# Random-feature attention and a gated MLP on one core: wider token chunks, and two sweeps over the weights in the second pass

## The chip, the cores and the metric

The kernel runs on one core of a Trainium2 chip. The metric is the device time of one execution in microseconds, as the median of several runs. TensorE (PE) does the matrix products, VectorE (DVE), ScalarE (ACT) and GpSimd (POOL) the element work, and SyncE (SP) issues most of the transfers between HBM and the on-chip memory SBUF. Products are summed in PSUM.

## The reference

```python
def _attn_ref(q, k, v, omega):            # q, k, v: 8 x 8 x 576 x 64, omega: 128 x 64
    def phi(x):
        proj = np.einsum('bhsd,md->bhsm', x, omega)
        h = proj - np.sum(x * x, axis=-1, keepdims=True) / 2.0
        h = h - np.max(h, axis=-1, keepdims=True)
        return np.exp(h) / np.sqrt(m)
    q_p, k_p = phi(q * scale), phi(k * scale)
    kv = np.einsum('bhsm,bhsd->bhmd', k_p, v)
    num = np.einsum('bhsm,bhmd->bhsd', q_p, kv)
    den = np.einsum('bhsm,bhm->bhs', q_p, np.sum(k_p, axis=2))[..., None] + 1e-06
    return num / den

x = attention, laid out as 4608 tokens x 512
gate = 1.0 / (1.0 + np.exp(-(x @ w_gate)))     # 512 -> 1536
val = x @ w_val                                # 512 -> 1536
out = gate * val @ w_out                       # 1536 -> 512
```

All of it is in fp32; the inputs arrive as float64.

## The kernel before

**Precision.** TensorE reads fp32r. Each operand is split into a high part (written by ACT) and a low part (input minus high, by DVE or POOL), and each product is three matmuls: low x high, high x low, high x high.

**Attention** takes some 500 us. It is a set of coroutines that are advanced in turn (`steps`). It leaves x, transposed, in DRAM (`xT`).

**Gated layer.** The 1536 columns are 12 tiles of 128, in 6 pairs. There are two ways of computing them. The *first pass* (`first_pass`, matmuls `gv` at L247) takes the first 4 tiles (pairs 0 and 1) for 9 chunks of 512 tokens, in plain products of 512 columns, 12 matmuls a step, 80 steps. Its steps are filler for attention: after every step attention is advanced RATE = 14 times. What is left of it when attention ends runs by itself. A chunk's operands are `xe`, a step's gate `ge` (ACT) and result `ye` (DVE). The *second pass* (`second_pass`, `gated`, matmuls `gw` at L351) takes the other 4 pairs in seven-product blocks (Strassen-Winograd): for each chunk of 512 tokens, each pair and each kind (gate, value) a *group* of 7 products of 6 matmuls, 256 columns wide. A product runs over one of seven combinations of quarters of x (`xl0` to `xl6`; sums `s3` to `s6` by DVE, high halves by ACT, low halves 0, 3 and 6 by POOL and 1, 2, 4 and 5 by DVE) and one of seven combinations of weights, a *unit* `u`. The sums of products are read from PSUM by ACT (`p1`) and DVE (`u2`, `u3`, `gl`, `yl`), multiplied and recombined by POOL and stored to DRAM as `yl`; the last group's multiplications are DVE's.

**Units.** Weights are converted from float64 during attention (`convert_weights`) and stored in DRAM as fp32 (`w32`), 1 MB each. `unit` loads one in two parts of 3 and 4 blocks and splits it (`u`, 128x768 and 128x1024). Units 0 to 7 of the second pass are all kept in SBUF for its whole length. Units 8 to 13 are the last layer's.

**Last layer** (`last`, matmuls `po` at L465): for 18 rows (c, s) of 2 x 128 tokens, and each pair j, 21 matmuls of 256 columns from `yh` and `yl`, which ACT and DVE split from the loaded `yr`. For pairs 0 and 1 four combinations of `yr` are first made by DVE (L456), since the first pass left plain products. The sums (`p1o`, `u2o`, `u3o`, `o`) are read by ACT and DVE.

**Order.** A scheduler orders each engine's instructions; those in `pin` keep the order in which the program was written. Every engine runs its instructions in order, and so a waiting one holds up those behind it. Buffers come from rings (`bufs=`); an `x` buffer for `xl`, `yh` and `yl` comes from a ring of 13.

Of the kernel before, what the change touches and what calls it, by code (L numbers as in the profile page):

```python
# [48 lines left out]
FROM = 20  # L49
RATE = 14  # L50
# [5 lines left out]
XK, XL = 5, 8  # L56
UL, UE = 5, 3
# [42 lines left out]
def attn_glu_kernel(ctx: ExitStack, tc, qT, kT, qn, kn, va, om, ident, w, out):  # L100
# [64 lines left out]

    def convert_weights(tiles, ns):

        for n in ns:
# [4 lines left out]
            b, t = f[:, :4], f[:, 4:]
            for o, x, y in (
                (t[:, 0], b[:, 3], b[:, 0]),
                (t[:, 2], b[:, 2], b[:, 3]),
                (t[:, 1], b[:, 2], t[:, 0]),
                (t[:, 3], b[:, 1], t[:, 1]),
            ):
                nc.gpsimd.tensor_tensor(out=o, in0=x, in1=y, op=ALU.subtract)  # L180
# [685 lines left out]
```

## Time and profile before

| | us |
|---|---|
| median of 3 runs | 1234.82 (1232.73 to 1238.44) |
| profiled execution | 1239.43 |
| its span in the profile | 1237.6 |

The span runs from the first to the last instruction. In the profile busy TensorE time is the sum of modelled matmul intervals; a group `L351 PE MATMUL gw<-xl,u ... x3024` names line, engine, operation, output and inputs with their count. In a timeline, the bracket `[3.57 <-ACT p L362]` is the idle time ahead and what ended it. The chain of waits is followed back from the last instruction. A window row gives start and end, length, then busy time and number of instructions of PE, weight load, DVE, ACT and POOL, the granted TensorE clock (1 is full), the DMA share and GB/s. TensorE's mean clock was 0.968.

### The profile page before, as it was taken

What the parts mean: (1) busy time and instruction counts of PE and PEld (TensorE: products, weight loads), DVE (VectorE), ACT (ScalarE), POOL (GpSimd) and SP (SyncE); (2) the same over time, 40 slices, a digit from 0 to 9 for tenths busy, and PEclk for the clock granted to TensorE, in tenths of its full rate; (3) what the DMA queues carried; (4) which work ended last, traced back from release to release, by engine and by line L of the source; (5) the groups of instructions that cost most, each with busy time, mean ns of one, the idle gap of its engine ahead of it and who ended that gap; (6) DMA issues with size and microseconds to landing.
All of it is one profiled execution on the core that took longest, in us unless ns stands there. A gap on an engine that the chain in (4) does not pass through costs nothing.

```text
span 1237.6 us, 23990 instructions
## 1 busy us (share of the span) xinstructions
PE 1172.3 (95%) x8828; PEld 1109.8 (90%) x8828; DVE 864.5 (70%) x1907; ACT 530.7 (43%) x1164; POOL 542.7 (44%) x599
## 2 busy tenths in 40 slices
PE   6798989999898999899899999999998899999998
PEld 5788978798887888788899999999998899999998
DVE  4889888999698866433566656666569777777773
ACT  5556755565455463342423322232325344343331
POOL 2454365556457552131466666666666211111110
PEclk7798989999899999899899999999999999999999
DMA  7667767786657641461432333323337676666662
GB/s 247 213 199 228 210 219 253 238 268 237 226 182 252 223 153 39 139 202 52 152 128 106 123 135 124 121 93 125 124 135 267 203 226 195 188 191 189 198 191 94
DMA packets 104950, 219.43 MB, mean 177 GB/s; under 512 B 11136, under 2 KB 42112, under 8 KB 103040
## 3 DMA queue, kind: packets, MB, share of 16 engines
q1 hardware_dynamic: 87984, 198.94, 48.5%
q10 hardware_dynamic: 16848, 18.95, 4.4%
q8 instruction: 70, 1.15, 0.4%
q14 instruction: 48, 0.39, 0.1%
HBM read 141.82 MB, written 76.02 MB: 176 GB/s over the span
## 4 chain that ended last, share of the span: by engine, by line
PE 71%; DVE 12%; issue 7%; DMA 5%; POOL 3%; ACT 1%; SPq 1%; ACTq 0%; DVEq 0%; POOLq 0%
PE gw L351 27%; PE po L465 20%; PE gv L247 10%; PE pkv L595 4%; PE pnq L638 4%; PE ptq L626 2%; DVE mxq L552 2%; DVE hq L615 1%; DMA xr<-xT 1%; DMA xT<-xsq 1%; DMA rawk<-kT 1%; POOL loq L71 1%; DVE hmq L556 1%; PE ppk L547 1%; POOL xe L71 1%
## 5 line engine op out<-in xcount | busy, mean ns | idle before, releaser
L351 PE MATMUL gw<-xl,u 128*128 128x256 f32 x3024 | 364.6, 283 | 6.9 <-ACT p L362 3.6
L351 PEld LDWEIGHTS gw<-xl,u 128*128 128x128 f32 x3024 | 363.5, 191 | 7.9 <-DVE u L331 3.9
L465 PE MATMUL po<-u,yh 128*128 128x256 f32 x1512 | 272.4, 283 | 0.0
L465 PEld LDWEIGHTS po<-u,yh 128*128 128x128 f32 x1512 | 234.8, 191 | 0.0
L465 PE MATMUL po<-u,yl 128*128 128x256 f32 x756 | 214.0, 283 | 3.3 <-DVE yl L71 3.3
L247 PE MATMUL gv<-xe,wh 128*128 128x512 f32 (+1 forms) x640 | 201.0, 388 | 2.1 <-POOL xe L71 2.1
L70 ACT ACTIVATE yh<-yr 128x896 fp32r<-128x896 f32 x108 | 100.2, 950 | 156.8 <-PE po L465 86.3
L465 PEld LDWEIGHTS po<-u,yl 128*128 128x128 f32 x756 | 144.3, 191 | 3.9 <-DVE yl L71 3.9
L247 PEld LDWEIGHTS gv<-xe,wh 128*128 128x128 f32 x640 | 117.3, 194 | 20.1 <-POOL xe L71 4.5
L71 POOL TENSOR_TENSOR yl<-yr,yh 128x896 fp32r<-128x896 f32 x17 | 38.0, 2232 | 215.3 <-PE po L465 139.9
L247 PE MATMUL gv<-xe,wl 128*128 128x512 f32 (+1 forms) x320 | 125.8, 394 | 2.7 <-POOL wl L71 1.6
L71 DVE TENSOR_TENSOR yl<-yr,yh 128x896 fp32r<-128x896 f32 x91 | 103.0, 1144 | 31.5 <-PE po L465 19.1
L331 DVE TENSOR_TENSOR u<-gw,p 128x256 f32<-128x256 f32 x144 | 60.7, 422 | 59.2 <-PE gw L351 51.1
L595 PE MATMUL pkv<-v,kpk 128*128 128x66 f32 x512 | 84.4, 290 | 13.3 <-ACT kpk L587 12.6
L595 PEld LDWEIGHTS pkv<-v,kpk 128*128 128x128 f32 x512 | 77.0, 209 | 21.5 <-ACT kpk L587 19.8
L71 POOL TENSOR_TENSOR lok<-rawk,hik 128x256 fp32r<-128x256 f32 (+1 forms) x80 | 55.5, 712 | 68.0 <-ACT hik L70 67.6
L456 DVE TENSOR_TENSOR yr<-yr 128x128 f32<-128x128 f32 x144 | 60.1, 451 | 35.3 <-DMA yr<-ye 34.8
L71 POOL TENSOR_TENSOR xe<-xr,xe 128x512 fp32r<-128x512 f32 (+1 forms) x40 | 49.1, 1244 | 74.2 <-ACT xe L70 62.4
L71 POOL TENSOR_TENSOR loq<-rawq,hiq 128x256 fp32r<-128x256 f32 (+1 forms) x80 | 56.5, 718 | 55.5 <-ACT hiq L70 54.7
L587 ACT ACTIVATE kpk<-ppk,nb 128x128 f32<-128x128 f32 x256 | 69.8, 393 | 17.4 <-DVE nb L574 17.1
L638 PEld LDWEIGHTS pnq<-kv,qpq 128*128 128x128 f32 (+1 forms) x640 | 70.5, 189 | 6.5 <-ACT qpq L628 4.3
L638 PE MATMUL pnq<-kv,qpq 128*128 128x66 f32 (+1 forms) x640 | 74.9, 273 | 1.4 <-ACT qpq L628 1.2
(108 smaller groups left out, 2166.6 us busy)
## 6 DMA issues: line engine op xcount, KB each, us to landing
yl<-yl SPq DMA_DIRECT2D x36, 896.0 KB, 3.8
yr<-yl SPq DMA_DIRECT2D x72, 448.0 KB, 3.5
xr<-xT SPq DMA_DIRECT2D x68, 256.0 KB, 4.7
c<-w SPq DMA_DIRECT2D x28, 512.0 KB, 5.1
w<-c SPq DMA_DIRECT2D x14, 1024.0 KB, 4.5
v<-va SPq DMA_DIRECT2D x32, 330.0 KB, 3.4
natk<-kn SPq DMA_DIRECT2D x36, 256.0 KB, 4.2
natq<-qn SPq DMA_DIRECT2D x36, 256.0 KB, 3.9
```

Source lines behind the costliest of these rows:

```text
L70: nc.scalar.activation(out=hi, in_=x, func=AF.Copy)
L71: (lo_engine or nc.vector).tensor_tensor(out=lo, in0=x, in1=hi.bitcast(F32), op=ALU.subtract)
L247: nc.tensor.matmul(gv, lhsT=u[:, s], rhs=v, start=(m == 0), stop=(m == 3 * KC - 1))
L331: return nc.vector.tensor_tensor(out=o, in0=a, in1=b, op=ALU.add)
L351: nc.tensor.matmul(o, lhsT=u[:, k, s], rhs=v[:, kc, :], start=(first and m == 0), stop=(m == 5), skip_group_check=not first,)
L456: nc.vector.tensor_tensor(out=raw[:, o], in0=raw[:, a], in1=raw[:, b], op=op)
L465: nc.tensor.matmul(o, lhsT=u[:, i, :], rhs=v[:, k, :], start=(j + m == 0 and n in (1, 6, 5, 4)), stop=(j == NPAIR - 1 and m == 2), skip_gr ...
L552: nc.vector.tensor_reduce(out=m.rearrange("p t h -> p (t h)"), in_=pp, axis=AX.X, op=ALU.max)
L587: nc.scalar.activation(out=kp[t][:, h, :], in_=pp[:, 2 * i + h, :], func=AF.Exp, bias=nb[:, t - t0, h : h + 1], scale=SCALE,)
L595: nc.tensor.matmul(pkv[:, h, :], lhsT=kp[b * MID + i][:, h, :], rhs=v[:, i, h, :], start=(i == 0), stop=(i == MID),)
L626: nc.tensor.transpose(out=pt[:, i, :], in_=h_sb[:, i, :], identity=id_sb)
L638: nc.tensor.matmul(pn[r, 2 * i + h, :], lhsT=qp[:, 2 * i + h, r], rhs=kvs[u, p, bb][:, h, :], start=True, stop=True,)
```

## The change

- The chunk of the second pass is 768 tokens instead of 512 (HC = 384 columns for a matmul, six chunks).
- The second pass is run in sweeps of two pairs each: sweep zero does pairs 0 and 1 on the last two chunks; then pairs 2 and 3, then pairs 4 and 5, each on all six chunks, 56 groups in all. Operands of x are so made 14 times for 768 tokens and not 9 times for 512.
- The first pass stops at 3072 tokens: 56 steps, 672 matmuls, and not 80 and 960.
- Only the four units of a sweep and one more are held. The next sweep's units are loaded in the last four groups of a sweep and split two groups later. Units -4 to -1 for sweep zero are put together again from the first pass's split weights, by POOL during attention (`first_units`), and stored in `w32`.
- Units 9 to 13 of the last layer come in the last four groups and behind them; unit 12 lies in three x buffers (`scattered`).
- RATE is 16 instead of 14, conversions start at first-pass step 14 instead of 20 (FROM), and the last layer has 8 x buffers.

The matmuls of the second pass go from 3024 of 256 columns to 2352 of 384; the last layer has 2268 before and after. Behind the last matmul of attention in TensorE's order stand 318 first-pass matmuls before and 72 after.

```diff
-NCH = B * S // NC
+HC = 384
+SUB = HC // P
+NC2 = B * S // (2 * HC)
+C0 = 4
+NCH = C0 * 2 * HC // NC
-FROM = 20
-RATE = 14
+FROM = 14
+RATE = 16
-XK, XL = 5, 8
-UL, UE = 5, 3
+XL, XT = 8, 4
...
+    def first_units(tiles):
+        for pair in range(EP):
+            for kind in range(2):
+                n = 2 * (pair - EP) + kind
+                f = tiles(f"z{pair}_{kind}")[:, : 4 * WP].bitcast(F32).rearrange("p (b q) -> p b q", q=Q)
+                for o, r, c in ((0, 0, 0), (1, 1, 0), (2, 1, 1), (3, 0, 1)):
+                    wh, wl = (t.bitcast(F32) for t in ws[2 * pair + c])
+                    i = (kind * KC + 2 * r) * P
+                    nc.gpsimd.tensor_tensor(out=f[:, o], in0=wh[:, i : i + Q], in1=wl[:, i : i + Q], op=ALU.add)
+                    if o % 2:
+                        yield
+                sums(f)
+                nc.sync.dma_start(out=w32[n % N_UNITS], in_=f)
+                yield
...
-        raw = load(c * NC, NC)
+        raw = load(c * 2 * HC, 2 * HC, late)
-        a11, a12, a21, a22 = raw[:, :2, :Q], raw[:, 2:, :Q], raw[:, :2, Q:], raw[:, 2:, Q:]
+        a11, a12, a21, a22 = raw[:, :2, :HC], raw[:, 2:, :HC], raw[:, :2, HC:], raw[:, 2:, HC:]
...
-        b0, b1, b2 = (any_bank(f"gw{i}_{id_}")[:, :Q] for i in range(3))
+        b0, b1, b2 = (any_bank(f"gw{i}_{id_}")[:, :HC] for i in range(3))
...
-        for c in range(NCH):
+        chunks = [(c, (j, j + 1)) for j in range(0, NPAIR, 2) for c in range(0 if j >= EP else C0, NC2)]
+        g_ = 0
+        for (c, pairs), after in zip(chunks, chunks[1:] + [None]):
...
-            if j < EP:
+            if j < EP and c < C0:
                 for o, a, b, op in ((3, 7, 2, ALU.add), (4, 3, 0, ALU.subtract), (5, 0, 7, ALU.subtract), (6, 1, 4, ALU.subtract)):
...
-        left = 2 * NE * (NCH + 1) - n
-        started, parts = [], iter(())
-        for n, _ in enumerate(gates):
-            if n == 2:
-                started = [unit(late, n) for n in range(UL)]
...
+        parts = operands(C0)
+        x = next(parts)
+        todo = [unit(late, n) for n in range(-2 * EP, 0)]
+        for one in todo:
+            next(one)
+        for _ in gates:
+            if todo:
+                next(todo.pop(0), None)
+            next(parts, None)
+            next(parts, None)
...
+    NZ, NA = 4 * (NC2 - C0), 4 * NC2
+    homes = {0: (0, tail)}
+    homes.update({NZ - 4 + i + 1: (i + 1, late) for i in range(4)})
+    homes.update({NZ + NA - 4 + i + 1: (i + 5, (tail, late, late, late)[i]) for i in range(4)})
+    homes.update({NZ + 2 * NA - 4 + i + 1: (i + 9, (late, tail, late, None)[i]) for i in range(4)})
+    for g in second_pass(x, parts):
+        if loading and loading[0][0] <= g:
+            next(loading.pop(0)[1], None)
+        if g in homes:
+            n, at = homes[g]
+            one = unit(at, n, both[n % 2]) if at else unit(late, N_LATE - 1, both[1])
+            next(one)
+            loading.append((g + 2, one))
+        if g == last_group - 1:
+            one = scattered(N_LATE - 2, nc.vector, nc.gpsimd, nc.vector)
```

Where the second pass begins, DVE's order before, up to the first reads of a second-pass sum (`u20_2_0`: kind 0, pair 2, chunk 0). Names end in a running number:

```order
L275 SCALAR_TENSOR_TENSOR ye4096_0_7642<-ge4096_0_7622,gv4096_0_1_7629 128x512
L300 TENSOR_TENSOR s0_3_7645<-xr0_0_7624 128x512
L300 TENSOR_TENSOR s0_4_7664<-s0_3_7645,xr0_0_7624 128x512
L275 SCALAR_TENSOR_TENSOR ye4096_1_7682<-ge4096_1_7662,gv4096_1_1_7669 128x512
L300 TENSOR_TENSOR s0_6_7705<-xr0_0_7624,s0_4_7664 128x512
L296 TENSOR_TENSOR xl0_4_7686<-s0_4_7664,xl0_4_7686 128x512
L296 TENSOR_TENSOR xl0_1_7688<-xr0_0_7624,xl0_1_7688 128x512
L275 SCALAR_TENSOR_TENSOR ye4096_2_7724<-ge4096_2_7703,gv4096_2_1_7711 128x512
L300 TENSOR_TENSOR s0_5_7727<-xr0_0_7624 128x512
L296 TENSOR_TENSOR xl0_5_7730<-s0_5_7727,xl0_5_7730 128x512
L275 SCALAR_TENSOR_TENSOR ye4096_3_7763<-ge4096_3_7745,gv4096_3_1_7750 128x512
L296 TENSOR_TENSOR xl0_2_7748<-xr0_0_7624,xl0_2_7748 128x512
```

The same place after (`xl4` belongs to chunk 4, the first of sweep zero; `u-2` and `u-1` are units, `u20_0_4` the first read):

```order
L344 TENSOR_TENSOR xl4_4_7257<-s4_4_7231,xl4_4_7257 128x768
L344 TENSOR_TENSOR xl4_1_7259<-xq3072_0_7179,xl4_1_7259 128x768
L217 TENSOR_TENSOR u-2_7190<-u-2_7190 128x768
L217 TENSOR_TENSOR u-2_7190<-u-2_7190 128x1024
L348 TENSOR_TENSOR s4_5_7286<-xq3072_0_7179 128x768
L212 SCALAR_TENSOR_TENSOR u-1_7193<-u-1_7193 128x768
L212 SCALAR_TENSOR_TENSOR u-1_7193<-u-1_7193 128x1024
L344 TENSOR_TENSOR xl4_5_7289<-s4_5_7286,xl4_5_7289 128x768
L344 TENSOR_TENSOR xl4_2_7292<-xq3072_0_7179,xl4_2_7292 128x768
L322 SCALAR_TENSOR_TENSOR ye2560_2_7343<-ge2560_2_7328,gv2560_2_1_7330 128x512
L322 SCALAR_TENSOR_TENSOR ye2560_3_7374<-ge2560_3_7359,gv2560_3_1_7361 128x512
L379 TENSOR_TENSOR u20_0_4_7388<-gw1_0_0_4_7385,p10_0_4_7387 128x384
```

Before, the units' halves stand 20 and more instructions earlier, among the first pass's `ye`, which alternate with the work on x. After, halves, work on x and the last two `ye` stand in one row ahead of the first read.

At the end of the second pass, DVE's order before, from the last sums of the last group to the last layer (`yl0_0_3` is the low half for c = 0, s = 0, j = 3):

```order
L331 TENSOR_TENSOR yl5_8_12315<-gw2_1_5_8_12387,u31_5_8_12390 128x2x128
L215 TENSOR_TENSOR u12_12304<-u12_12304 128x768
L331 TENSOR_TENSOR yl5_8_12315<-gw1_1_5_8_12386,p11_5_8_12388 128x2x128
L331 TENSOR_TENSOR yl5_8_12315<-gw2_1_5_8_12387,u21_5_8_12389 128x2x128
L385 TENSOR_TENSOR yl5_8_12315<-yl5_8_12315,gl5_8_12314 128x2x128
L386 TENSOR_TENSOR gl5_8_12314<-yl5_8_12315,gl5_8_12314 128x256
L387 TENSOR_TENSOR yl5_8_12315<-yl5_8_12315,gl5_8_12314 128x2x128
L215 TENSOR_TENSOR u13_12378<-u13_12378 128x768
L215 TENSOR_TENSOR u13_12378<-u13_12378 128x1024
L71 TENSOR_TENSOR yl0_0_3_12566<-yr0_0_3_12471,yh0_0_3_12565 128x896
```

And after:

```order
L379 TENSOR_TENSOR yl5_5_11144<-gw1_1_5_5_11213,p11_5_5_11215 128x3x128
L379 TENSOR_TENSOR yl5_5_11144<-gw2_1_5_5_11214,u21_5_5_11216 128x3x128
L433 TENSOR_TENSOR yl5_5_11144<-yl5_5_11144,gl5_5_11143 128x3x128
L434 TENSOR_TENSOR gl5_5_11143<-yl5_5_11144,gl5_5_11143 128x384
L435 TENSOR_TENSOR yl5_5_11144<-yl5_5_11144,gl5_5_11143 128x3x128
L217 TENSOR_TENSOR u10_11207<-u10_11207 128x768
L217 TENSOR_TENSOR u10_11207<-u10_11207 128x1024
L217 TENSOR_TENSOR u11_11272<-u11_11272 128x768
L232 TENSOR_TENSOR u12_0_11275<-u12_0_11275 128x768
L232 TENSOR_TENSOR u12_2_11277<-u12_2_11277 128x256
L75 TENSOR_TENSOR yl0_0_2_11394<-yr2_11210,yh0_0_2_11393 128x896
```

Before, `u10`, `u11` and `yl0_0_2` stood ahead of these rows, so only `u12` and `u13` were left; after, `u10` to `u12` stand between the last group and `yl0_0_2`.

A few instructions on, DVE's order at the second row (0,1) of the last layer before:

```order
L456 TENSOR_TENSOR yr0_1_0_12659<-yr0_1_0_12659 128x128 x4
L456 TENSOR_TENSOR yr0_1_1_12692<-yr0_1_1_12692 128x128 x3
L71 TENSOR_TENSOR yl0_1_0_12668<-yr0_1_0_12659,yh0_1_0_12667 128x896
L331 TENSOR_TENSOR u2o0_0_12641<-po1_0_0_12479,p1o0_0_12640 128x256
L331 TENSOR_TENSOR o0_0_0_12643<-po0_0_0_12478,p1o0_0_12640 128x256
L331 TENSOR_TENSOR u3o0_0_12642<-po1_0_0_12479,u2o0_0_12641 128x256
```

And after:

```order
L379 TENSOR_TENSOR u2o0_0_11494<-po2_0_0_11333,u2o0_0_11494 128x256
L379 TENSOR_TENSOR o1_0_0_11497<-po2_0_0_11333,u3o0_0_11495 128x256
L379 TENSOR_TENSOR o0_0_0_11496<-po2_0_0_11333,u2o0_0_11494 128x256
L379 TENSOR_TENSOR o1_0_0_11497<-po3_0_0_11334,u3o0_0_11495 128x256
L509 TENSOR_TENSOR yr0_1_0_11512<-yr0_1_0_11512 128x128 x2
L509 TENSOR_TENSOR yr0_1_1_11545<-yr0_1_1_11545 128x128 x4
L75 TENSOR_TENSOR yl0_1_0_11521<-yr0_1_0_11512,yh0_1_0_11520 128x896
```

The low half that row (0,1) begins with stood ahead of the sums of row (0,0), and now stands behind them and behind all the combinations of `yr`.

More of the change, by code (lines that the diff above doesn't have):

```diff
@@ L197, in unit, with place @@
+    def place(at, n):
+        u = at.tile([P, 2, N_OPS, Q], F32R, tag="u", bufs=4 if at is late else 1, name=f"u{n}")
+        units[n] = [[u[:, i, k] for k in range(N_OPS)] for i in range(2)]
+        return u
+    def unit(at, n, lo_engine=None):
+        u = place(at, n)
         whole = u[:, 1].bitcast(F32)
         keep_order = pin if lo_engine else lambda x: x
-        keep_order(nc.sync.dma_start(out=whole[:, :3], in_=w32[n, :, :3]))
-        keep_order(nc.sync.dma_start(out=whole[:, 3:], in_=w32[n, :, 4:]))
+        keep_order(nc.sync.dma_start(out=whole[:, :3], in_=w32[n % N_UNITS, :, :3]))
+        keep_order(nc.sync.dma_start(out=whole[:, 3:], in_=w32[n % N_UNITS, :, 4:]))
@@ L269, in first_pass @@
                 yield
-                if parts and at is late:
-                    ahead += [t for t in (next(parts, None),) if t]
                 val = product(1, j, o, n, x)
@@ L411, in second_pass @@
                     next(group)
+                    if pair == pairs[0] and kind:
+                        assert next(parts, parts) is parts
+                        if after:
+                            parts = operands(after[0])
+                            ahead = next(parts)
+                    else:
+                        next(parts, None)
                     next(held, None)
@@ L736, in attn_glu_kernel @@
                 n += 1
-                if next(conv, conv) is conv and n >= FROM:
-                    next(later, None)
+                if next(conv, conv) is conv:
+                    next(again, None)
+                    if n >= FROM:
+                        next(later, None)
+            for _ in again:
+                pass
             for _ in later:
@@ L789, in attn_glu_kernel @@
-    for c in range(NCH):
-        for s in range(Q // P):
+        parts = operands(C0)
[6 more added lines that the diff above has]
+                next(todo.pop(0), None)
+            next(parts, None)
+            next(parts, None)
+        for one in todo:
+            next(one, None)
+    tail = ctx.enter_context(tc.tile_pool(name="tail", bufs=1))
+    both = (nc.vector, nc.gpsimd)
@@ L791, in attn_glu_kernel @@
+    last_layer = True
+    for c in range(NC2):
+        for s in range(SUB):
             for _ in last(c, s, raws):
```

222 lines of the change are left out of this document (108 added, 114 removed).

## The prediction

> **What bounds the kernel now.** I read the page first (busy shares, then the chain of waits), then the windows of each stage, then the timelines of TensorE where one stage hands over to the next, and last the groups of instructions of the two engines that feed it.
>
> ```profile
> PE 1172.3 (95%) x8828; PEld 1109.8 (90%) x8828; DVE 864.5 (70%) x1907; ACT 530.7 (43%) x1164; POOL 542.7 (44%) x599
> PE 71%; DVE 12%; issue 7%; DMA 5%; POOL 3%; ACT 1%; SPq 1%; ACTq 0%; DVEq 0%; POOLq 0%
> ```
>
> TensorE is busy for 95% of the span. The windows (busy time and count of each engine, granted clock, DMA share, GB/s) split that by stage: attention with first-pass filler, rest of the first pass, start of the second pass, its steady part, its end with the start of the last layer, and the last layer.
>
> ```profile
> 120.00:508.00 388.00, 364.28 (x2601) 324.06 (x2599) 318.56 (x822) 211.26 (x584) 192.81 (x226) 0.97 0.60 202
> 508.00:585.50 77.50, 76.34 (x322) 61.48 (x322) 24.83 (x30) 26.87 (x42) 18.54 (x14) 0.97 0.44 146
> 585.50:597.00 11.50, 7.93 (x64) 7.72 (x63) 4.55 (x7) 4.85 (x7) 0.00 (x0) 0.91 0.81 247
> 590.00:597.00 7.00, 3.43 (x26) 3.22 (x25) 2.00 (x3) 2.93 (x5) 0.00 (x0) 0.85 0.97 295
> 597.00:600.00 3.00, 3.00 (x16) 3.00 (x15) 2.25 (x7) 1.79 (x2) 0.00 (x0) 0.50 0.87 343
> 597.00:930.00 333.00, 333.00 (x2778) 333.00 (x2777) 203.57 (x435) 97.98 (x192) 215.75 (x255) 0.99 0.32 121
> 930.00:958.00 28.00, 24.71 (x200) 23.97 (x199) 27.47 (x44) 16.69 (x24) 17.11 (x16) 1.00 0.80 266
> 958.00:980.00 22.00, 18.74 (x140) 18.13 (x139) 17.27 (x28) 6.25 (x9) 6.62 (x5) 0.92 0.65 210
> 980.00:1237.60 257.60, 252.91 (x2119) 252.70 (x2117) 179.48 (x330) 96.74 (x117) 37.95 (x17) 1.00 0.61 185
> ```
>
> The steady second pass leaves TensorE no gap at all (333.00 of 333.00 us), with DVE at 61% and POOL at 65% behind it. So only two things can move the time: what TensorE's matmuls cost, and how long it stands still at the hand-overs. The rows of the chain give the price of a matmul (start, length, what, count):
>
> ```profile
> 522.18 63.34 PE gv L247 x275
> 587.10 7.76 DMA u<-w
> 594.88 1.06 ACT u L214
> 596.27 333.12 PE gw L351 x2772
> 979.44 251.72 PE po L465 x2106
> ```
>
> A matmul of 256 columns takes 333.12/2772 = 120.2 ns (119.5 in the last layer). One of 512 takes 63.34/275 = 230.3 ns with the waits in that stretch, and without them, by the period of three in TensorE's timeline, 0.68/3 = 226.7 ns:
>
> ```profile
> 578.77 0.62 PE L247 MATMUL gv<-xe,wh 128*128 128x512 f32 x2
> 579.45 0.62 PE L247 MATMUL gv<-xe,wh 128*128 128x512 f32 x2
> ```
>
> Doubling the columns adds 106.5 ns, so some 13.7 ns are paid for each instruction whatever its width.
>
> **The matmuls.** No row has one of 384 columns. From above it is bounded by the 256-column rate for each column, 1.5 x 120.2 = 180.3 ns; from below by the 512-column rate, 0.75 x 226.7 = 170.0 ns. Both rows are equally near, so I take the line through them, 173.5 ns. Second pass before: 3024 x 120.2 ns = 363.5 us. After: 2352 x 173.5 ns = 408.1 us (336 of them are the new sweep over tile pairs 0 and 1 on two chunks). The order has 318 first-pass matmuls behind the last one of attention before and 72 after; 246 x 226.7 ns = 55.8 us go. Sum 408.1 - 363.5 - 55.8 = **-11**; the ends are -19 (170.0 ns) and +5 (180.3 ns). The 2268 matmuls of the last layer stay.
>
> The Trainium skill ("TensorE: Matmul & The Clock Gate", section "Back-to-back issue gap") has an isolated warm gap of N/2.4 + 2.5 ns, and warns that a stream may differ from it; worked out that is 109.2, 162.5 and 215.8 ns at 256, 384 and 512 columns, hardly a fixed cost, and -1.1 us for the sum instead of -11. The rows above are 11 ns longer than this at both widths, which is just the fixed cost that I count, so the trace does not agree.
>
> **Attention.** There 42 of the 642 first-pass matmuls go: 42 x 226.7 ns = 9.5 us if TensorE sets the pace. It is busy 94% of the stretch 120 to 508. Against it stand 32 new POOL operations of 256 elements, which rebuild four weight units from the split halves, at the price of the same operation in the conversions:
>
> ```profile
> L180 POOL TENSOR_TENSOR c<-c 128x256 f32<-128x256 f32 x56 | 44.7, 818 | 1.7
> ```
>
> 32 x 0.818 = 26.2 us on an engine busy 192.81 of 388 us; and four stores of 1 MB, which SP issues among attention's loads. POOL also makes the low halves that TensorE waits for in attention. Ends: -9.5 (all hidden) and +10 (three quarters of the 26.2 us on the path). POOL has half its time free, so I take **-7**.
>
> **Hand-over 1, first pass to second pass.** TensorE's first long stop, and ACT's wait that ends just before it:
>
> ```profile
> 594.88 1.06 ACT L214 ACTIVATE u<-u 128x1024 fp32r<-128x1024 f32 x1 [4.01 <-DMA u<-w]
> 596.27 4.04 PE L351 MATMUL gw<-xl,u 128*128 128x256 f32 x17 [3.57 <-ACT p L362]
> ```
>
> ACT stood in order behind the late load of unit 5. Before costs 3.6 us of stop and 1.5 us at half clock (0.50 in 597 to 600) there. After, five units in front of the second pass become four (u-4 to u-1), but the 318 matmuls (73 us) that hid loads, sums and halves are 72 (16.6 us). The memory of attention comes free at its end E, so all loads start there: 1.57 MB of x and four units of 0.92 MB, 5.2 MB, at 295 GB/s (row 590 to 597) 18 us. DVE works through the halves, sums and lows in program order, and puts the last two first-pass products (ye2560_2, ye2560_3, 0.688 each) and the first read of a second-pass sum (u20_0_4) behind all of them. Prices of its operations:
>
> ```profile
> L215 DVE TENSOR_TENSOR u<-u 128x768 fp32r<-128x768 f32 x7 | 6.7, 953 | 4.3 <-ACT u L214 4.3
> L215 DVE TENSOR_TENSOR u<-u 128x1024 fp32r<-128x1024 f32 x6 | 8.4, 1406 | 7.0 <-ACT u L214 6.9
> L209 DVE SCALAR_TENSOR_TENSOR u<-u 128x1024 fp32r<-128x1024 f32 x2 | 3.5, 1762 | 0.0
> L275 DVE SCALAR_TENSOR_TENSOR ye<-ge,gv 128x512 f32<-128x512 f32 x14 | 9.6, 688 | 46.1 <-PE gv L247 37.8 <-ACT ge L268 5.3 <-issue 2.9
> ```
>
> From u-4 on: four unit halves of 768 and eight operations on x of 768, 12 x 0.953 = 11.4; two halves of 1024 at 1.41 and two scaled ones at 1.76, 6.3; two ye, 1.4: 19.1 us. u-4 lands behind 2.5 MB, at E + 8.4, its high half takes ACT one more microsecond: DVE is through at about E + 28.5. TensorE runs out of first-pass work at E + 16.6, has four products of 6 matmuls (4.2 us) that can run meanwhile, and then needs what u20_0_4 frees: a stop of 7 to 8 us, and 1.5 us at half clock, 9 against 5: **+4**. Ends: -5 (lows and halves in time, the old stop gone too) and +12 (DVE's operations longer beside POOL, below).
>
> The Trainium skill (same page, "What's actually happening") has the clock halved after a window of some 3.4 us idle and whole again after one busy. The 0.50 behind 3.57 us agrees, and by it stops shorter than that cost no clock; the stop of 2.23 us in hand-over 2 below, with a mean clock of 0.92 around it, does not agree. Nothing in the sum hangs on it.
>
> **The steady part and the two sweep changes.** Rows of 597 to 930 for what DVE and POOL do, and the one price of a POOL low of 1024 (930 to 985):
>
> ```profile
> L331 DVE TENSOR_TENSOR u<-gw,p 128x256 f32<-128x256 f32 x133 | 56.1, 422 | 57.1 <-PE gw L351 49.1 <-ACT p L362 7.8
> L385 POOL TENSOR_TENSOR yl<-yl,gl 128x256 f32<-128x256 f32 x33 | 33.1, 1002 | 80.8 <-issue 39.1 <-ACT p L362 21.1 <-ACT xl L293 20.5
> L391 POOL TENSOR_TENSOR yl<-yl 128x256 f32<-128x256 f32 x33 | 24.3, 738 | 0.0
> L296 POOL TENSOR_TENSOR xl<-s,xl 128x512 fp32r<-128x512 f32 x16 | 20.8, 1300 | 0.0
> L296 DVE TENSOR_TENSOR xl<-s,xl 128x512 fp32r<-128x512 f32 x16 | 15.3, 956 | 0.0
> L300 DVE TENSOR_TENSOR s<-s,xr 128x512 f32<-128x512 f32 x8 | 5.5, 683 | 0.0
> L215 POOL TENSOR_TENSOR u<-u 128x1024 fp32r<-128x1024 f32 x2 | 5.2, 2608 | 7.1 <-ACT u L214 7.1
> ```
>
> A chunk after has two pairs, 168 matmuls, 29.1 us. DVE has 22 reads of sums; by the step from 422 (256) to 688 ns (512, ye above) one of 384 takes 0.555: 12.2 us; and eight operations on x of 768, 0.953 alone or, stretched as 956 is over 683, 1.34: 7.6 to 10.7. That is 68 to 79%. POOL has 14 products (0.738 to 1.002 at 256, so 1.0 to 1.4 by the step to 1300) and three lows of 768 at 1.9 (between 1.3 and 2.6): 19.7 to 25.3, 68 to 87%. Neither bounds the steady part: 0. At each sweep change (groups 7 to 10, 31 to 34) four units arrive within one chunk: DVE gets four halves of 768 and two of 1024, 6.6 us more, POOL two of 1024, 5.2 us. Then DVE stands at 91 to 101% and POOL at 86 to 105%, on work that comes in bursts, with the next chunk's x queued behind the units' halves on both and TensorE waiting for that x. I take 3 us for each change, **+6**; ends 0 (the means of 597 to 930 hold and bursts fit) and +14 (both at the upper shares, and half clock behind each stop).
>
> **Hand-over 2, second pass to last layer.** TensorE's stops there before, one of DVE's halves, and two of DVE's groups from the page:
>
> ```profile
> 941.68 10.39 PE L351 MATMUL gw<-xl,u 128*128 128x256 f32 x84 [1.41 <-DVE u L331]
> 953.44 0.98 PE L351 MATMUL gw<-xl,u 128*128 128x256 f32 x6 [1.37 <-DVE u L331]
> 966.39 0.38 PE L465 MATMUL po<-u,yl 128*128 128x256 f32 x1 [2.23 <-DVE yl L71]
> 975.92 0.39 PE L465 MATMUL po<-u,yl 128*128 128x256 f32 x1 [0.24 <-DVE yl L71]
> 957.21 2.83 DVE L215 TENSOR_TENSOR u<-u 128x768 fp32r<-128x768 f32 x1
> L71 DVE TENSOR_TENSOR yl<-yr,yh 128x896 fp32r<-128x896 f32 x91 | 103.0, 1144 | 31.5 <-PE po L465 19.1
> L456 DVE TENSOR_TENSOR yr<-yr 128x128 f32<-128x128 f32 x144 | 60.1, 451 | 35.3 <-DMA yr<-ye 34.8
> ```
>
> The windows from 930 to 980 miss 3.3 + 3.3 = 6.6 us of TensorE, and the clock of 0.92 another 1.5: 8 us. Before, units 8 to 13 came in over eight groups of the last chunk. After there are four; DVE's halves of units 9 to 12 and the reads of the last group stand together, and yl0_0_2, which TensorE needs after two blocks of 21 (5.0 us) of the last layer, comes behind two sums, three products, u10, u11a and two parts of u12: 2 x 0.555 + 3 x 0.555 + 0.953 + 1.406 + 0.953 + 0.953 + 0.422 + 1.1 = 8.6 us alone (the row of 957.21 shows one of 768 at 2.83, beside POOL). So TensorE stops 4 to 5 us there. Unit 13 and three yr are fetched only after the last product, 2.3 MB, 8 us at 295 GB/s, just in time behind that stop. Then row (0,1): before, yl0_1_0 stood ahead of the sums of (0,0) on DVE (stop 0.24); now it stands behind eight of them and all eight combinations of yr, and the last sum waits for the last matmul of (0,0): six combinations of 0.45 at best, one sum 0.42 and 1.1, some 4 us of stop. With the sums of the last group (as before, 2.8), half clock (1.5) and late loads (2) that makes some 15 against 8: **+7**. Ends 0 (the new stops replace the old) and +14 (DVE at that 2.83).
>
> In the last layer 48 of 144 combinations go from DVE and its x buffers fall from 13 to 8, four blocks ahead of TensorE (10 us); TensorE bounds it (252.91 of 257.60): 0.
>
> **Sum.** -11 - 7 + 4 + 6 + 7 = -1, from 1239.43 in the profiled execution to 1238.4. That execution lay 4.6 us over the median of 1234.82, so I forecast 1234 for the median. 0.5% (6.2 us) is about what a measurement can tell from no change here.
>
> **The rivals.**
> Faster, the covers hold: the three hand-over terms are zero, since DVE and POOL still idle a quarter of the time, and the old stops are merely moved; the two gains stay: 1234 - 17 = 1217. For it: TensorE loses just 13 us at hand-overs before. Against it: the order of DVE above, which has a fixed queue behind late loads.
> Slower, DVE and POOL hold each other up in every chunk: two operations that read SBUF lengthen each other (956 against 683; 2.83 against 0.953). It decides from where DVE's eight x operations reach 29.1 - 12.2 = 16.9 us, 2.1 us each, 2.2 times the lone price. At 2.4 times, 1.4 us in each of 14 chunks: +19, 1253. Against it: 597 to 930 shows a factor of 1.4 only.
> The Trainium skill ("SBUF — State Buffer", section "Who interferes with whom") has this pair exclude each other; the lengthened rows agree, and the price above is theirs.
> Slower, attention pays for the rebuilding: +10 in place of -7: 1251. Against it: POOL half idle.
> Slower, a matmul pays for its columns alone: 180.3 ns, +5 in place of -11: 1250. Against it: the 226.7. The gap of the Trainium skill ("Back-to-back issue gap", above) goes the same way and would give 1244.
>
> **How the numbers follow.** The forecast, with its own range of 1226 to 1242, 0.40, a fifth of it below 1228.6; covers hold 0.30; DVE against POOL 0.16; attention 0.08; columns 0.06. Faster 0.30 + 0.08 = 0.38, slower 0.16 + 0.08 + 0.05 = 0.29, same 0.33. The range reaches from 1212 (covers hold, matmuls at 171 ns) to 1255 (DVE against POOL).
>
> **What would show it.** Right: the second pass's matmuls in the chain at 173 to 174 ns; a stop of 7 to 8 us for DVE behind the first products of the first sweep; stops of 2 to 4 us about its two changes; and two of 4 to 5 us on yl at the start of the last layer. Wrong: no stop over 2 us at the changes or hand-overs (faster), waits for xl in every chunk (slower), or attention's end moved by more than 10 us from 508.

## The result and the profile after: 5% slower

| | before | after |
|---|---|---|
| median of 4 runs, us | 1233.78 (1230.44 to 1238.44) | 1295.72 (1291.16 to 1300.20) |
| ratio to before | | 1.050, 95% interval 1.045 to 1.055 |
| profiled execution, span, clock | 1239.43, 1237.6, 0.968 | 1296.65, 1294.7, 0.949 |

The forecast was 1234, no change. First the busy shares and the chain of waits of the page after:

```profile
PE 1178.4 (91%) x7868; PEld 1115.4 (86%) x7868; DVE 925.3 (71%) x1803; ACT 568.7 (44%) x1152; POOL 637.5 (49%) x583
PE 33%; DVE 11%; POOL 10%; issue 7%; DMA 6%; SPq 1%; ACT 1%; DVEq 0%; POOLq 0%; ACTq 0%
```

TensorE's busy time rose by 6 us. The two chains can't be compared by these shares: after, the chain can be followed back only to 408 us, so its shares sum to 69% of the span. Taken from the first to the last matmul of the second pass alone, TensorE has 89% of the chain before and 23% after, POOL 26% and DVE 22%: there the chain now runs through DVE and POOL. The windows show where (columns as before: length, then PE, weight load, DVE, ACT, POOL, then the granted clock, DMA share, GB/s). They are the rest of the first pass, the start of sweep zero, the two sweep changes with a steady stretch behind each, and the start of the last layer in two parts:

```profile
510.25:527.50 17.25, 16.53 (x74) 13.36 (x72) 5.25 (x5) 6.27 (x9) 2.08 (x1) 1.00 0.78 281
527.50:548.00 20.50, 9.41 (x31) 8.54 (x32) 18.06 (x18) 9.07 (x12) 4.93 (x3) 0.70 0.30 99
610.00:648.00 38.00, 32.77 (x158) 31.94 (x159) 29.45 (x36) 14.54 (x22) 30.70 (x20) 0.83 0.37 135
680.00:770.00 90.00, 88.11 (x492) 85.40 (x491) 56.41 (x85) 30.58 (x44) 63.57 (x51) 1.00 0.38 145
806.00:845.00 39.00, 33.02 (x158) 32.39 (x159) 29.82 (x36) 14.71 (x22) 31.32 (x20) 0.84 0.36 133
876.00:995.00 119.00, 116.60 (x648) 112.36 (x648) 77.33 (x122) 39.23 (x57) 81.54 (x65) 1.00 0.39 146
995.00:1016.00 21.00, 9.96 (x66) 9.73 (x67) 20.61 (x20) 13.80 (x16) 13.80 (x7) 0.78 0.90 327
1016.00:1034.00 18.00, 13.67 (x90) 13.50 (x89) 12.19 (x23) 3.85 (x5) 0.77 (x1) 0.78 0.41 130
```

Before, the steady part had 333.00 of 333.00 us busy. Now even there TensorE stands for 2% of the time (88.11 of 90, 116.60 of 119); at the two sweep changes it stands 5 to 6 us and the clock falls to 0.83 and 0.84, and at the last layer's start it stands 15 of 39 us at 0.78. TensorE's longest stops, from its timeline (the bracket is the idle time ahead and what ended it), and two steady chunks:

```profile
534.60 5.30 PE L399 MATMUL gw<-xl,u-4_7184 128*128 128x384 f32 x17 [3.17 <-DVE xl L344]
545.48 2.26 PE L399 MATMUL gw<-xl,u-4_7184 128*128 128x384 f32 x6 [5.57 <-DVE u L379]
610.43 2.29 PE L399 MATMUL gw<-xl,u 128*128 128x384 f32 x7 [2.02 <-ACT p L410]
643.78 34.07 PE L399 MATMUL gw<-xl,u 128*128 128x384 f32 x179 [4.20 <-DVE xl L344]
878.54 30.15 PE L399 MATMUL gw<-xl,u 128*128 128x384 f32 x168 [0.36 <-ACT p L410]
909.04 30.27 PE L399 MATMUL gw<-xl,u 128*128 128x384 f32 x168 [0.35 <-ACT p L410]
1014.59 0.58 PE L518 MATMUL po<-u,yl 128*128 128x256 f32 x1 [10.94 <-DVE yl L75]
1031.75 0.55 PE L518 MATMUL po<-u,yl 128*128 128x256 f32 x1 [4.33 <-DVE yl L75]
```

A chunk of 168 matmuls comes every 30.5 us (878.54 to 909.04). The width is not to blame. In a stretch without a wait 24 weight loads, one for each matmul, start one after the other within 4.20 us; less the last one's own length (193 ns on the page) that is 174 ns each, 29.2 us for 168:

```profile
689.84 4.20 PEld L399 LDWEIGHTS gw<-xl,u 128*128 128x128 f32 x24
```

From the starts of the matmuls in the trace, each chunk's time less 168 x 174 ns is a loss of 18.0 us in the first chunk, 11.4 and 12.5 in the two chunks at the sweep changes, 1.2 to 2.6 (18.0 together) in the ten other chunks and 3.7 in the last: 63.6 us in all. Two of the ten, 4.2 us of the 18.0, lie behind the chunks at the changes and have no stop, only slower matmuls. Of the 63.6 us some 39 are stops (starts over 0.6 us apart) and some 14 are matmuls at half clock, which start every 320 ns instead of 174; the rest is shorter waits. Before, at 119.2 ns for a matmul, the loss was 6.5 in the first chunk, 6.1 in the last and nothing between. The stages of the two spans add up to the difference of 57.1 (attention ends here with the end of its last matmul):

| stage | before | after | change | forecast |
|---|---|---|---|---|
| to the end of attention | 508.4 | 510.3 | +1.8 | -7 |
| rest of the first pass | 76.9 | 16.2 | -60.7 | -55.8 |
| second pass, first to last matmul | 372.8 | 472.7 | +99.9 | +54.6 with hand-over 1 and sweep changes |
| from there to the end | 279.5 | 295.6 | +16.1 | +7, with the last group's waits |

In a steady chunk the wait that starts it is one instruction of DVE. DVE and POOL from one of them, with TensorE's stop:

```profile
767.06 0.96 DVE L348 TENSOR_TENSOR s<-xq,s 128x768 f32<-128x768 f32 x1 [4.76 <-POOL xl L344]
764.21 1.01 POOL L439 TENSOR_TENSOR yl<-yl 128x384 f32<-128x384 f32 x1
765.18 1.84 POOL L344 TENSOR_TENSOR xl<-s,xl 128x768 fp32r<-128x768 f32 x1
768.94 2.21 PE L399 MATMUL gw<-xl,u 128*128 128x384 f32 x11 [0.81 <-DVE xl L344]
```

The sum s6 is written into the buffer that s3 had (the ring has two). POOL's low half of x3 still reads s3, and stands in order behind the products of a pair. DVE stands 4.76 us, with two low halves and the reads of PSUM behind it. In the kernel before, a chunk's operands had eight groups to be made in, here four. The same wait of s6 stands in all thirteen chunks that are made during another, 2.2 to 5.2 us long, and 5.21 ahead of the stops of 4.20 and 4.02 at the sweep changes. The chain of this chunk also runs through 7.01 us of loading x (748.25 to 755.26): the load starts only when DVE has made the last low half of the chunk before, since x as loaded has a single buffer (`xq`). A second one there was not tried.

### The profile page after: what moved, and what is told of

Read it like the earlier page. It is cut to its first block, busy times and chain, and to the rows that moved or that the text cites. A ratio compares the mean times of both kernels' runs of the same rounds, so it can differ in the third digit from the quotient of the medians.

```text
span 1294.7 us, 21829 instructions
## 1 busy us (share of the span) xinstructions
PE 1178.4 (91%) x7868; PEld 1115.4 (86%) x7868; DVE 925.3 (71%) x1803; ACT 568.7 (44%) x1152; POOL 637.5 (49%) x583
## 4 chain that ended last, share of the span: by engine, by line
PE 33%; DVE 11%; POOL 10%; issue 7%; DMA 6%; SPq 1%; ACT 1%; DVEq 0%; POOLq 0%; ACTq 0%
PE po L518 21%; PE gw L399 8%; DMA xq<-xT 4%; POOL xl L344 3%; DVE s L348 2%; DVE xl L344 2%; POOL yl L439 1%; PE pnq L691 1%; PE gv L301 1%; DVE u L379 1%; POOL yl L436 1%; POOL yl L437 1%; POOL yl L435 1%; POOL gl L434 1%; DVE gl L379 1%
## 5 line engine op out<-in xcount | busy, mean ns | idle before, releaser
L399 PE MATMUL gw<-xl,u 128*128 128x384 f32 x2016 | 372.8, 345 | 20.9 <-DVE xl L344 11.0
L399 PEld LDWEIGHTS gw<-xl,u 128*128 128x128 f32 x2016 | 360.8, 193 | 32.5 <-DVE xl L344 16.1
L518 PEld LDWEIGHTS po<-u,yh 128*128 128x128 f32 x1512 | 238.2, 194 | 0.0
L301 PE MATMUL gv<-xe,wh 128*128 128x512 f32 (+1 forms) x448 | 142.9, 389 | 6.4 <-POOL xe L75 6.4
L379 DVE TENSOR_TENSOR u<-gw,p 128x384 f32<-128x384 f32 x112 | 62.1, 555 | 58.0 <-PE gw L399 40.5
L341 ACT ACTIVATE xl<-s 128x768 fp32r<-128x768 f32 x56 | 47.3, 844 | 122.5 <-DVE s L348 122.5
L301 PEld LDWEIGHTS gv<-xe,wh 128*128 128x128 f32 x448 | 82.2, 199 | 16.9 <-POOL xe L75 9.2
L648 PE MATMUL pkv<-v,kpk 128*128 128x66 f32 x512 | 82.4, 286 | 11.8 <-ACT kpk L640 11.5
L301 PE MATMUL gv<-xe,wl 128*128 128x512 f32 (+1 forms) x224 | 88.3, 396 | 4.9 <-POOL wl L75 4.7
L640 ACT ACTIVATE kpk<-ppk,nb 128x128 f32<-128x128 f32 x256 | 69.5, 390 | 20.5 <-DVE nb L627 19.7
L344 POOL TENSOR_TENSOR xl<-s,xl 128x768 fp32r<-128x768 f32 x28 | 61.1, 2183 | 30.0 <-ACT xl L341 30.0
```

Of the source, the lines that this page charges most:

```text
L301: nc.tensor.matmul(gv, lhsT=u[:, s], rhs=v, start=(m == 0), stop=(m == 3 * KC - 1))
L341: pin(nc.scalar.activation(out=b[:, 0], in_=a, func=AF.Copy))
L344: pin(engine.tensor_tensor(out=x[n][1], in0=of[n], in1=x[n][0].bitcast(F32), op=ALU.subtract))
L379: return nc.vector.tensor_tensor(out=o, in0=a, in1=b, op=ALU.add)
L399: nc.tensor.matmul(o, lhsT=u[k][:, s], rhs=v[:, kc, :], start=(first and m == 0), stop=(m == 5), skip_group_check=not first,)
L518: nc.tensor.matmul(o, lhsT=u[:, i, :], rhs=v, start=(j + m == 0 and n in (1, 6, 5, 4)), stop=(j == NPAIR - 1 and m == 2), skip_group_check ...
```

## The experiments

Ratios are to the kernel before on the same chip; that of the changed kernel is 1.050 (1.045 to 1.055). Kernels with the changed kernel's attention unchanged ended it (here the start of its last weight load, 0.4 to 0.6 us ahead of the end used above) anywhere from 505.7 to 513.0 us in their profiles, so small differences of whole times are read from the stages.

**A third buffer for s (s3).**

```diff
-            s = late.tile([P, 2, HC], F32, tag="s", bufs=2, name=f"s{c}_{n}")
+            s = late.tile([P, 2, HC], F32, tag="s", bufs=3, name=f"s{c}_{n}")
...
```

> Edit: the ring of the sums s has three buffers instead of two (the space comes from a tile that is only needed at the start). Queue theory: on DVE the sum s6 waits in every chunk for the buffer of s3, which POOL's low half of x3 still reads behind seven products (4.76 us in one chunk of the trace after), and DVE's reads of PSUM queue behind it. Then the loss of 1.2 to 2.5 us in each of eleven steady chunks falls below 0.5, and the last stops at the two sweep changes (4.2 and 4.0) go: 20 to 25 us, 1271 to 1276. Load theory: DVE and POOL have too much to do and hold each other up, whatever the order; a third buffer moves the wait elsewhere, within 5 us of 1296.

The last layer's output tiles lie in the same ring and have three buffers too. Ratio 1.041 (1.037 to 1.044), 1287.5 us. s6 waits in no chunk any more. The chunks that have no unit near lost 0.6 to 1.5 us instead of 1.2 to 2.6. At the changes the 11.4 and 12.5 became 5.3 and 6.4, but the chunks behind them went from 1.9 and 2.3 to 5.8 and 5.0, and the second chunk of sweep zero from 2.0 to 4.2. The stop that came in its place, and POOL ahead of it:

```profile
648.93 94.10 PE L400 MATMUL gw<-xl,u 128*128 128x384 f32 x521 [3.85 <-POOL xl L345]
647.06 3.59 POOL L345 TENSOR_TENSOR xl<-s,xl 128x768 fp32r<-128x768 f32 x2
```

The queue theory holds in the steady part, for half of the loss: the seven chunks that have no unit near lost 5.9 us together instead of 11.8. There too DVE and POOL now lengthen each other: from 680 to 800 us DVE's low halves took 1.36 (from s) and 1.72 us (from x) on average, and 0.95 and 1.00 in the changed kernel. At the changes the load theory has its share: DVE no longer stands, so POOL's seven products ahead of x3's low half take 10.7 us (636.36 to 647.06) instead of 8.6 (631.45 to 640.07), and that low half is itself late. Half of the expected gain came.

**Units -2 and -1 later (defer).**

```diff
+        second, todo = todo[2:], todo[:2]
...
     for g in second_pass(x, parts):
+        if second:
+            next(second.pop(0), None)
```

> Edit: the halves of units -2 and -1 are made after the first and second group of sweep zero instead of ahead of it. Queue theory: some 6 us of halves go from DVE's queue ahead of the first reads of PSUM; the loss of 18 us in the first chunk falls to about 10, so 1288. Load theory: the halves only move into a chunk in which DVE is busy anyway, 1294 or more.

Ratio 1.043 (1.039 to 1.047), 1292.3 us; the first chunk lost 15.2 instead of 18.0. The stop of 5.57 became 1.54, but the one of 1.08 at the chunk's end became 2.80 (s6 waits 4.15 us there, and 2.24 in the changed kernel), and two other waits of that stretch stayed: unit -4 lands 12 and 13 us after attention's end at 281 GB/s, and the sums s3, s4 and the low half of x4 follow one another on DVE only from there (stops 2.29 and 3.17). A cover of 16.2 us is too short for that chain, whatever stands behind it.

**Units 11 to 13 between the blocks of the last layer's first row (lastly).**

```diff
-            for _, one in loading:
-                next(one, None)
...
-            for _ in last(c, s, raws):
-                pass
+            for j, _ in enumerate(last(c, s, raws)):
+                if loading and j:
+                    next(loading.pop(0)[1], None)
```

> Edit: the halves of units 11, 12 and 13 are made one at a time between the blocks of the last layer's first row instead of all ahead of it; this also puts the low halves of the second row ahead of the sums of the first on DVE. Queue theory: the stops of 10.9 and 4.3 us at the start of the last layer, and the half clock behind them, shrink to 5 us or less together: 12 us, 1284. Rival (transfers): unit 13 and three yr land late behind 327 GB/s of traffic, and TensorE waits as long for those: 1293 or more.

Ratio 1.042 (1.038 to 1.046), 1288.4 us; from the last second-pass matmul to the end 288.8 us and not 295.6, so 6.8 us of the 12 expected. The stops are 5.96 and 3.57 now, still over the 5 expected. DVE and POOL of the changed kernel in this place:

```profile
1002.37 5.38 DVE L217 TENSOR_TENSOR u<-u 128x768 fp32r<-128x768 f32 x3
1007.68 4.24 DVE L232 TENSOR_TENSOR u<-u 128x768 fp32r<-128x768 f32 x2
1011.85 2.69 DVE L75 TENSOR_TENSOR yl<-yr,yh 128x896 fp32r<-128x896 f32 x1
1008.58 3.06 POOL L217 TENSOR_TENSOR u<-u 128x1024 fp32r<-128x1024 f32 x1
1011.59 1.99 POOL L232 TENSOR_TENSOR u<-u 128x768 fp32r<-128x768 f32 x1
1013.55 3.21 POOL L217 TENSOR_TENSOR u<-u 128x1024 fp32r<-128x1024 f32 x1
```

Units' halves and the low half that TensorE waits for take some twice their lone time beside POOL: 2.69 for one of 896 beside POOL's 1.99 and 3.21, and 1.08 for each of the next three, behind POOL's last. The order was a cause, the transfers were not: DVE had no idle time from 1000.04 us to this low half, unit 13 and the three yr had landed by 1012.42, and DVE took them up only at 1014.46 and 1017.51.

**Dummy matmuls in the stops (warm).**

```diff
+        warm(b1, {(C0, 0, 0): 10, (1, 2, 0): 20, (1, 4, 0): 20}.get(at, 0))
         product(6, b1, True)
...
+            if (c, s) == (0, 1):
+                rewarm(28)
+            for j, _ in enumerate(last(c, s, raws)):
+                if raws and j == 1:
+                    rewarm(70)
```

> Edit: the changed kernel with dummy matmuls, whose result is not used, put in front of matmuls that stand still: 10 of 384 columns in the first group of sweep zero, 20 in the first group of the second chunk of each later sweep (stop of 4.2 and 4.0 us in the trace after), 70 of 256 ahead of the third block of the last layer (stop 10.9) and 28 ahead of its second row (stop 4.3). Each lot is shorter than the stop it stands in. Clock theory: a good part of the loss is the half clock that follows each stop of 2 us and more, some 61 us at half clock between the start of the second pass and the last layer; with the stops filled about half of those stretches go, and 8 to 14 us with them: 1282 to 1288. Rival: the stops alone are the loss, and TensorE catches up behind them anyway: within 3 us of 1296, or slower by the dummies' own time, 1300.

Ratio 1.039 (1.035 to 1.042), 1288.9 us: some 1.1%, although TensorE does more. In its profile the second pass is 2.1 us shorter and the rest 4.6, together 0.5%. The same windows of this kernel, the second sweep change and the last layer's start:

```profile
806.00:845.00 39.00, 36.30 (x188) 35.02 (x188) 29.54 (x35) 15.00 (x21) 31.61 (x20) 0.91 0.34 130
995.00:1016.00 21.00, 18.34 (x137) 18.12 (x136) 20.65 (x17) 12.59 (x16) 14.69 (x7) 0.92 0.79 298
1016.00:1034.00 18.00, 17.97 (x150) 17.76 (x150) 13.13 (x27) 5.88 (x7) 0.27 (x1) 1.00 0.59 188
```

The clock was 0.91, 0.92 and 1.00 there instead of 0.84, 0.78 and 0.78. From the start of the second pass to the end of the last matmul the time at half clock fell from 61 to 31 us (10 in the kernel before). The half clock behind a stop is a loss of its own, but a smaller one than the stop: by the starts of the matmuls, those at half clock cost 19.7 us over their full-clock time in the changed kernel, beside 54.5 us of stops (4.1 and 10.8 in the kernel before), and 11.4 us here.

**The three together, and with dummies (all3, all3warm).** Edits: s3, defer and lastly in one; then dummies in the stops that are left.

> Edit: third buffer for s, units -2 and -1 later, units 11 to 13 between the blocks, together. Queue theory: the three effects lie in different places and add, 1.04 per cent, 0.6 and 0.8: ratio 1.024 to 1.028 to the kernel before. Load theory: DVE and POOL are the bound in the stretches in which units are split, so part of the gain of one is lost in the next: 1.033 or more.

> Edit: the three changes of order and ring together, and dummy matmuls in the stops that are left there (10 ahead of the second product of sweep zero, 17 and 13 ahead of the third product of the second chunk of each later sweep, 40 and 24 ahead of the third and fourth block of the last layer). If stops and half clock are separate losses, this takes half of the 37 us at half clock that are left, 5 to 9 us: ratio 1.020 to 1.023. If the order changes already took what the clock can give: 1.026 or more. Either way slower than before, since the chunks at sweep changes still lose 5 to 6 us each.

Ratios 1.027 (1.023 to 1.031), 1273.9 us, and 1.029 (1.026 to 1.032), 1274.5 us. The three add, as the queue theory has it: 2.3% against 0.9, 0.7 and 0.8. With dummies the half clock fell from 37 to 17 us, and the time did not follow: the stage from the last second-pass matmul to the end took 290.8 us against 290.7. The dummies paid in the long stops of the changed kernel and gave nothing in the shorter ones that are left here; why was not tested.

**All low halves of units on DVE (all3d).**

```diff
-    both = (nc.vector, nc.gpsimd)
+    both = (nc.vector, nc.vector)
```

> Edit: as the three changes together, but all low halves of units on DVE, none on POOL, at the sweep changes. The stops of 3.8 and 3.0 us there now end with POOL's low half of x3. If POOL alone is late, 5.2 us less for it in each change takes these two stops away, 6 to 10 us with the half clock: 1.020. If DVE and POOL hold each other up, the sum of their work counts and DVE's reads come later instead: 1.025 to 1.030.

Ratio 1.027 (1.024 to 1.030), 1271.1 us. The stop on POOL's low half of x3 at the first change fell from 3.84 to 2.01, and a new one of 0.97 on DVE's u came. The gain of the first theory did not come. That fits the second, that at the changes the sum of DVE's and POOL's work is too much, but no run shows that alone.

**A unit's halves a group apart (spread).**

```diff
+            if o.start == 0:
+                yield
```

> Edit: at the sweep changes the two halves of a unit are made one group apart, the first a group earlier than now. Queue theory: ACT's two copies of a unit (1.78 us) stand ahead of the read of the first product (stop of 2.0 at both changes), and DVE's two halves (3.7 us) ahead of its reads; one half at a time lets the reads through, so the loss of 11.4 and 12.5 us at the changes falls to 8 each: 1288. Load theory: POOL and DVE have the same work in the same chunk and the loss stays at 11 to 13: 1294 to 1297.

Ratio 1.044 (1.040 to 1.049); the chunks at the changes lost 11.2 and 11.4 us. No effect there: the load theory's side. (Its profile ended attention at 505.7, the early end of the scatter.)

**Attention: the rebuilding, FROM and RATE (norebuild, from17, nore17, rate14, before16).**

```diff
-                    nc.gpsimd.tensor_tensor(out=f[:, o], in0=wh[:, i : i + Q], in1=wl[:, i : i + Q], op=ALU.add)
...
-FROM = 14
+FROM = 17
...
-RATE = 16
+RATE = 14
```

> Edit: the 32 POOL operations that rebuild units -4 to -1 are left out; as many bytes are stored from the split weights (so sweep zero computes with other weights). If POOL's rebuilding holds attention up, attention ends some 9 us earlier than at 510, and the time is 1287. If attention's end is set by its own chain and by the higher RATE, it moves by 3 us at most, 1293 to 1297.

> Edit: the changed kernel with FROM 17 instead of 14. If the conversions that start three steps earlier crowd DVE and POOL in the middle of attention, attention ends 8 to 15 us earlier: ratio 1.038 to 1.044. If the rebuilding sets it, the end stays within 4 us: 1.046 to 1.053.

> Edit: the changed kernel with FROM 17 and without the 32 POOL operations that rebuild four units (sweep zero computes with other weights). If FROM and the rebuilding each cost attention some 13 us but hide each other, this ends attention 14 to 18 us earlier, as the kernel before with RATE 16 does: ratio 1.035 to 1.039. If something else in the change holds attention up, such as the four stores, it stays over 1.045.

> Edit: the changed kernel with RATE 14, so that 36 and not 72 first-pass matmuls are left when attention ends. If attention's end is not set by the number of filler matmuls (no gain from 42 fewer was seen), it stays at 510 plus or minus 3, the rest of the first pass is 8 us shorter, but the first chunk of sweep zero loses as much more, since its loads start at attention's end: 1293 to 1298. If filler does set the pace, attention ends 8 us later and the time is 1302 or more.

And in the kernel before, RATE 16 and FROM 17:

> Edit: the kernel before with RATE 16 and conversions started at step 17, so that attention has 600 first-pass matmuls in it and not 642, as in the changed kernel, and 360 are left. If filler sets the pace of attention, attention ends 9 us earlier and the rest takes 9 us longer: the same time, and then the changed kernel lost 9 us in attention to something else. If attention has a pace of its own, its end stays at 508 plus or minus 3 and the time is 1.006 to 1.009.

| kernel | ratio | attention ends at |
|---|---|---|
| before | 1 | 507.8 |
| before16 | 0.994 (0.991 to 0.997) | 491.8 |
| changed | 1.050 (1.045 to 1.055) | 509.8 |
| rate14 | 1.052 (1.048 to 1.056) | 527.1 |
| norebuild | 1.048 (1.044 to 1.052) | 511.1 |
| from17 | 1.046 (1.042 to 1.049) | 508.7 |
| nore17 | 1.041 (1.039 to 1.043) | 506.0 |

RATE 16 (with FROM 17) is worth 16 us of attention in the kernel before, where 9 or none were expected, for some 10 us more behind it, and 17 us in the changed kernel (rate14 is the undoing of it), where 8 were. So the rate of the filler sets attention's pace up to 16, and the change took from attention what RATE gave: 17 to 19 us at equal RATE. Part of it stands in the windows from 60 to 120 of before16, of the changed kernel and of norebuild:

```profile
60.00:120.00 60.00, 53.06 (x408) 50.02 (x409) 51.47 (x135) 37.24 (x104) 31.21 (x35) 0.89 0.68 223
60.00:120.00 60.00, 46.77 (x335) 43.16 (x334) 45.87 (x112) 32.35 (x94) 43.23 (x51) 0.83 0.58 191
60.00:120.00 60.00, 50.79 (x393) 48.01 (x394) 49.47 (x127) 34.15 (x98) 29.50 (x33) 0.91 0.78 257
```

With the rebuilding POOL has 43.2 us instead of 31.2 there, and TensorE gets 335 matmuls done instead of 408; without it 393. From the start to 120 us they are 567, 610 and 595. But norebuild lost the lead again after 200 us and ended attention no earlier, where 9 us were expected of the rebuilding; from17 gained 1 us, where 8 to 15 were expected if FROM was the cause; both together brought the end to 506.0, 4 us earlier and within the scatter. What holds attention up, the four stores or the order that the scheduler makes of it, was not found; some 14 us stay open.

**The kernel before with two small edits (beforelate, before16late, before18late).** Units 5 to 7 are split two groups later; then RATE 16 and FROM 17, or 18 and 15, with it.

```diff
-        elif started:
+        elif started and (c, g) > (0, 1):
             next(started.pop(0))
```

> Edit: the kernel before, with the halves of units 5 to 7 made two groups later, so that ACT doesn't stand behind their loads when it has the first products to read. The stop of 3.6 us and the half clock behind it (6.8 us long) go: 0.3 to 0.5 per cent, ratio 0.995 to 0.997, faster than both kernels. Rival: the wait moves to the next group that needs the unit, 0.999 to 1.002.

> Edit: the kernel before with RATE 16, conversions from step 17, and the halves of units 5 to 7 two groups later. The two gains lie in different stages and add: 0.994 times 0.9965, 0.990. If the second was only the clock phase of a run, 0.994.

> Edit: the same with RATE 18 and conversions from step 15. If attention gives back more than the filler that it loses at any RATE, 0.986 to 0.988. If RATE 16 is about where filler only fills stops, moving 40 more matmuls behind attention costs 9 us and gives less: 0.991 to 0.996.

Ratios 0.997 (0.995 to 0.998), 0.990 (0.988 to 0.993) and 1.006 (1.003 to 1.009); times 1234.4, 1225.2 and 1243.3 us. In the first, ACT reads the second group's first product before it waits for unit 5, and the window behind kept its clock (1.00, against 0.50 from 597 to 600 in the kernel before):

```profile
590.80 0.38 ACT L362 ACTIVATE p<-gw 128x256 f32<-128x256 f32 x1
594.27 1.06 ACT L214 ACTIVATE u<-u 128x1024 fp32r<-128x1024 f32 x1 [2.36 <-DMA u<-w]
597.00:604.00 7.00, 6.20 (x49) 5.87 (x48) 6.89 (x11) 4.84 (x8) 3.58 (x4) 1.00 0.44 170
```

before16late is 1.0% faster than the kernel before; the two gains add, as expected. RATE 18 lies outside both of its expected ranges: it ended attention at 491.5, no earlier than RATE 16 (491.8), with 54 more matmuls behind it, so there attention has a pace of its own.

## Why the prediction was wrong, step by step

- **The matmuls, -11.** Right: 174 ns where the line gave 173.5, and 60.7 us less behind attention where 55.8 were counted; -12 in all. Neither the rule that has hardly any fixed cost nor the rate by columns (180.3) held.
- **"Neither bounds the steady part: 0".** This step failed: +18 us, of which 4 are half clock left over from the sweep changes. It compared shares (DVE 68 to 79%, POOL 68 to 87%) with 100%, and the shares came out no higher than forecast: 56.41 of 90 and 63.57 of 90, 63% and 71%. What it did not look at was that one instruction of DVE waits for one of POOL in each chunk through a ring of two. s3 took that wait away and with it half of the steady loss; the other half stays open.
- **Sweep changes, +6.** This step failed by as much: measured +24. The upper shares of over 90% were in the text; taking 3 us for each gave a burst no queue and no clock. In the trace the wait of s6 is longest here (5.21), and one low half in each change took DVE 2.38 and 2.39, where the steady ones take 0.95 to 1.06. So of the rivals, "DVE and POOL hold each other up" named a mechanism that was there, but priced it for every chunk; which part each has at the changes stays open.
- **Hand-over 1, +4.** The chunk lost 18.0 against 6.5, +11.5. The stops were 2.3, 3.2 and 5.6 us, with two more of 0.8 and 1.1, where one of 7 to 8 was forecast; some 4 us are slower matmuls where 1.5 was counted. u-4 was all there at E + 13.1 and not E + 8.4, in part since the loads began only 3 us behind attention's end, and DVE was through at E + 34.5 and not E + 28.5.
- **Hand-over 2, +7.** Measured +16.1 together with the rest of the last layer. The two stops stood in the named places on DVE's low halves, at 10.94 and 4.33 us: the first was forecast at 4 to 5, by lone durations, and DVE ran at half speed beside POOL there, as the quoted 2.83 had shown. "Transfers in time" was right.
- **Attention, -7.** Measured +1.8. What the lower number of matmuls gives was under-counted (9.5, and 16 in before16), and what the change costs there was more so (17 to 19). Against the text, the rebuilding is not shown to be that cost: it costs time up to 120 us, and without it attention ended no earlier. Which step failed here stays open.
- **Half clock.** The sum has it at the hand-overs, 1.5 us each, and not at the changes; the trace has 61 us of it in eight stretches, which cost 19.7 us. The Trainium skill ("TensorE: Matmul & The Clock Gate", section "What's actually happening") ties it to an idle window of about 3.4 us; here stops of 2.0 us were followed by it (610.43, clock 0.83 in the window), so by this trace shorter stops are not free.

The measured terms are -12 for the matmuls, +2 for attention, +11.5, +18, +24, -2 for the last chunk and +16: 57 us. All five terms that rested on cover erred to the same side, and the range, which was built with one rival at a time, was too narrow. The signs that the prediction gave for being right did not tell it from this: the matmul of 174 ns and stops of 2.0 and 4.2 us at the changes came as named, and the time did not.

## What to carry to other kernels

When a change halves the time in which side work must be done, follow each wait of that work through its rings and queues; a share of 70% does not say that it fits. Price a stop of TensorE of 2 us or more above its own length, for the half clock behind it: here 19.7 us came to 54.5 us of stops. And before restructuring, try the numbers that the change also moves: here the filler's rate, with the start of the conversions and the halves of three units moved, made the old kernel 1.0% faster.

## What the runs showed of the hardware

- A matmul of 384 fp32r columns started every 174 ns, on the line between 120 (256) and 227 (512): some 12 to 14 ns were paid for each at these three widths. At half clock it was 320 ns for 384 columns and 213 for 256, which is 0.83 ns a column at both, with nothing to spare for a fixed part.
- Stops of 2.0 us could be enough for the clock to halve, for 3.4 or 6.8 us at a time and 13.7 in the stop of 10.94; short dummy matmuls in long stops kept it at 0.91 to 1.00 and gained 1.1% (0.5% in the stages of the profile).
- A low half of 896 elements took 2.69 us on DVE beside POOL's halves, against 1.08 alone; POOL's half of 1024 took 3.06 and 3.21 there, against 2.37 at 610 us: both lengthen.
